# The second batch's attention turned through DRAM and multiplied by quarters of the array

## Chip, cores and metric

One core of a Trainium2 chip runs the whole program. The metric is the device time of one execution in microseconds (us); lower is better. The kernel before takes 828.4 us (median of 3 runs, 827.59 to 828.51).

## What is computed

A softmax-like attention without a score matrix, then a feed-forward layer over all its tokens (8 batches, 8 heads, 576 tokens, 64 dims a head; model width 512, inner width 2048):

```python
q_s = exp(q - max(q, axis=-1)); q_s = q_s / (sum(q_s, axis=-1) + 1e-09)
k_s = exp(k - max(k, axis=2));  k_s = k_s / (sum(k_s, axis=2) + 1e-09)
kv  = einsum('bhsd,bhse->bhde', k_s, v)
x   = einsum('bhsd,bhde->bhse', q_s, kv)        # then (4608, 512) tokens
h   = x @ w_in;  g = s * max(h, 0)**2 + b;  out = g @ w_out
```

q, k, v and w_in are drawn eight times larger than in a plain layer; everything is float32.

## The kernel before

**Attention.** The work is cut in units of two heads (`u`, four a batch) and pairs of units (`pr`, two a batch). A unit's tokens lie on 128 partitions as four full groups and a fifth, half-full one: the 64 left tokens of a head. For x, the dims of q have to lie on partitions, so q is turned. Batches 0 and 1 (`k_stream`, `k_pair`, `q_stream`, `q_left`, `kv_stream`, `kv_second`) do this on TensorE: `qT` transposes the four full groups of a unit (L543), `xp` multiplies them by `kvf` (L553), a 128x128 matrix with the two heads' kv on its diagonal blocks; the left tokens of a pair go through `qTl` (L603) and `xpl` (L610). In batch 1 the maximum of k over the tokens is also found with TensorE: `kT` turns the partial maxima (L629) and `mb` spreads the result over the partitions (L636). Batches 2 to 7 (`k_late`, `k_exps`, `q_late`, `kv_late`, `x_late`) keep those turns away from TensorE: VectorE transposes 32x32 blocks (L763), SyncE stores the result to DRAM (`turned`, L766) and loads it back in another order (L771), ScalarE and VectorE split it in a high and a low part, and `xp` is three fp32r products for each half (L830). The maxima of k go through DRAM in the same way (L679, L683).

**The layer.** For batches 0 to 4 it goes in 16 steps of 128 inner columns (`step`): `h` (L1468, 12 products of 128x512), then r, gh and gl on ScalarE and VectorE, then `acc` (L1548, 12 products of 128x512). Each of the 80 steps is 24 such products on TensorE. In the first block of steps the weights are also fetched (L291, L293) and brought into a high and a low part on ScalarE and VectorE (`conv_w`: `low`, `st`, `w`; L307 to L326). Batches 5 to 7 and the left tokens of all batches go through a scheme with seven products instead of eight (`product` L1104, `second` L1195); it is not touched.

**Order.** Every piece of work is a generator that yields an `Op` (engine, planned cost, due time, needs, buffers). A table of letters, `TURNS_TAKEN`, says which generator comes next, so the order of the instructions on each engine is fixed when the program is built; each engine works through its own list in order. Where the plan leaves TensorE idle at the start, `idle` (L1691) puts in transposes without a use (`unused`, L1702). The plan's costs are not times of the chip. SyncE issues nearly all transfers, in order: one that waits holds back all behind it.

The lines that say what a late unit does on TensorE:

```python
qs = part().rearrange("p l (s a n c) -> p l s n a c", s=2, a=2, c=SQ)
for s_, n in enumerate((NT, NQ)):
    for k, (l, m) in enumerate(((0, 0), (1, 0), (0, 1))):
        nc.tensor.matmul(xp[:, s_, 0:n * D], kv_part()[:, l, i], qs[:, m, s_, 0:n], start=k == 0, stop=k == 2)
```

Of the kernel before, what the change touches and what calls it, by code (L numbers as in the profile page):

```python
# [9 lines left out]
F32 = mybir.dt.float32  # L10
# [16 lines left out]
def attention_moe(ctx: ExitStack, tc: tile.TileContext, q, k, v, w_in, w_out, s, b, out):  # L27
# [4 lines left out]
    P = 128  # L32
# [29 lines left out]
    DUE_Q = (-17.0, -5.5, -20.5, -11.0, 8.5, 5.5, 12.5, 14.0)  # L62
    DUE_V = (-13.5, -19.0, -11.5, 14.0)
# [63 lines left out]
    class Op:  # L127
# [11 lines left out]
        "aaaaababaaaaabaaabaWabaWabaQaWaWabaQaWaQabaWaXaWaQabaXaRaQaWauaRaXabaXaWabaRaXaba8aRaXabaXavabaRabauaSavabaua8avaSabauabaSaYaoauaSa8aYaZaTaS"  # L139
        "aqauaWaYaZaYaTaXaWaYaTaZbcaYaWaYaZa9aTaXaZbcaXaTawaZaYaZaXa9awaYaXawavaZbcaZa9adbcawavaYadaxaZavaeaYaxaeacaZbcaYawaZbcbcacayawbcbcaye1axbdbc"  # L140
        "bda4bcaxbda4aybdbcafaxafa4aybdbcbdbcaxagbdbcagaUbcbdbeaUaybebda4beazayapbeaAbda4e2a4bdazbea4bdaAazbdbeaAa4bfazbfbeaAbfa4ahaza4ahbfbea4aiaDaU"
        "azbeaibfbeaDaAbebfbeaDaAbgbfbgaDe3aBbgaCbfbgakaDaBbfakaCa1bgbfaDaBbfaCbfbgaEbhaBbgbhaCbgaBbhajaCbhajaBbgaCbhe4a1bgaFbha1bga1aEbgbha1biaEbhbi"
        "a1bia1aGbiaEa1bibhaUalbiaFbhalaGbibha0bibha0a1aUbibja0aEaUbjaFaEbjbjaGaUbiaFaJbibjbiaJaUambjbiaJamaGbkbjbkaUaJanbkaFbjanbaa5aJaFa5aGbkarbaaK"
        "babjaJbaa5bjaKataGbjaKbkbjaKaHblbkaKblaHbkaKe5blaHbkblaIaHbkblaIbkaHblaIbkaHblbkaIe6a0bmblaIbma0asa5aIbmaNa0a1a0aLa5bma1a5aNblbma5a1blbmaVa0"
        "bmblaVbmblaLa0bnbmaNa0aNaLbna0bnaMa0bnaNaLa5bmaMbnaNbma5aLa5bnaMbma5aLbmbnaMe7boaObnboaMaOaPboaMaOaPboa2aPaVaObnboaVbnboaPaVboa2bnaVa2bnboaV"
        "bpaOaPbpboaVaObpaVaPbpe8a2a3bobpa2a3bobpa2boa2bpboa3bqbpa3a2bpbqa3a2bqa3a3bqbpbqeQeQbpbqbpbqbpbqa3bbbqa3brbbcubrbbbbbrcva2cwbra2bqa2brcxbqbr"
# [12 lines left out]
        "fud1dmbVbUeAd0fubWd1bWeAfubWd1fufubWfubVbWekbWeUd2bWbVd2cVekbWbVekbWbVekeUbXekdmbXbXcUdmdEbXd0dEcWbWbXd0bWdFbXd1bWd2dFbWbXd2bYbXeZbYd2bYd2bY"
# [406 lines left out]
    def q_left(pr):  # L566
# [1192 lines left out]
```

## Time and profile before

| what | value |
|---|---|
| median of 3 runs | 828.4 us (827.59 to 828.51) |
| the profiled execution, its time | 828.27 us |
| its span, first to last instruction | 826.5 us |
| TensorE busy | 817.6 us, 4301 records |
| VectorE busy | 673.3 us |
| ScalarE busy | 463.5 us |
| GpSimd busy | 205.3 us |
| granted TensorE clock | 1.00 of full speed in every slice |

PE is TensorE, DVE VectorE, ACT ScalarE, POOL GpSimd, SPq the queue of SyncE. A float32 product (not fp32r) shows as two records, so `xp` of L553, two products a unit, counts x4. The records of neighbouring products overlap, since they are pipelined: how long one keeps TensorE is read from start to start, and the chain of waits prints just that.

### The profile page before, as it was taken

Reading aid. Unit: us, or ns where it says so; the run is one execution under the profiler, and the core shown is the slowest. Engines: PE = TensorE matmul, PEld = TensorE weight load, DVE = VectorE, ACT = ScalarE, POOL = GpSimd, SP = SyncE. Lnnn points to the kernel's source line nnn. Section 1 sums busy time; section 2 is a strip of 40 time slices with the busy share of each in tenths; the row PEclk is TensorE's granted clock in tenths of the full one; section 3 lists DMA queues with packets and bytes.
Section 4 is the critical chain, followed back from the end, with each engine's and each line's share of the span. In section 5 each row is a group of like instructions: output and inputs, shape, how many; then the busy total and the mean of one; then the engine's idle time right before and its main releaser. Section 6 shows DMA issues by size and latency. Waiting matters only on the chain.

```text
span 826.5 us, 12888 instructions
## 1 busy us (share of the span) xinstructions
PE 817.6 (99%) x4301; PEld 676.7 (82%) x4301; DVE 673.3 (81%) x1155; ACT 463.5 (56%) x768; POOL 205.3 (25%) x206
## 2 busy tenths in 40 slices
PE   8999999999999999999999999999999999999997
PEld 7688888888888888888888888888888888888886
DVE  6999956799899996978979978699969976656883
ACT  4999964356446455564556555545447644445650
POOL 3100012212212122222222322335342005353500
PEclk9999999999999999999999999999999999999999
DMA  9999523587867666866695754789889967666314
GB/s 267 319 375 318 164 70 110 151 228 191 218 179 198 168 170 205 214 177 144 203 241 163 242 149 149 231 264 283 276 253 325 251 156 214 203 182 187 90 18 73
DMA packets 217206, 165.64 MB, mean 200 GB/s; under 512 B 91444, under 2 KB 200500, under 8 KB 217140
## 3 DMA queue, kind: packets, MB, share of 16 engines
q1 hardware_dynamic: 212116, 163.83, 68.6%
q10 hardware_dynamic: 5024, 0.98, 0.6%
q8 instruction: 34, 0.56, 0.3%
q14 instruction: 32, 0.26, 0.1%
HBM read 112.85 MB, written 52.44 MB: 200 GB/s over the span
## 4 chain that ended last, share of the span: by engine, by line
PE 96%; DVE 2%; issue 1%; ACT 0%; POOL 0%; POOLq 0%; ACTq 0%
PE acc L1548 27%; PE h L1468 26%; PE bankU L1104 11%; PE overX L1195 8%; PE bankV L1104 8%; PE overY L1195 5%; PE overZ L1195 5%; PE xp L830 2%; PE kv L402 2%; PE kT L440 1%; PE xp L553 1%; PE unused L1702 0%; PE bankU L1195 0%; DVE low L318 0%; DVE st L311 0%
## 5 line engine op out<-in xcount | busy, mean ns | idle before, releaser
L1468 PE MATMUL h<-x,w 128*128 128x512 f32 x960 | 238.2, 392 | 1.3 <-ACT r L1500 0.8
L1468 PEld LDWEIGHTS h<-x,w 128*128 128x128 f32 x960 | 177.9, 188 | 38.8 <-ACT r L1500 1.3
L1548 PE MATMUL acc<-w,gh 128*128 128x512 f32 x640 | 199.2, 392 | 0.0
L1548 PEld LDWEIGHTS acc<-w,gh 128*128 128x128 f32 x640 | 118.1, 188 | 23.5
L1548 PE MATMUL acc<-w,gl 128*128 128x512 f32 x320 | 125.1, 391 | 0.1
L1500 ACT ACTIVATE r<-h 128x512 f32<-128x512 f32 x80 | 47.9, 599 | 94.7 <-PE h L1468 94.1
L1104 PE MATMUL bankU<-w,ring 128*128 128x512 f32 x378 | 95.9, 389 | 0.0
L1104 PEld LDWEIGHTS bankU<-w,ring 128*128 128x128 f32 x378 | 70.9, 188 | 14.7
L1548 PEld LDWEIGHTS acc<-w,gl 128*128 128x128 f32 x320 | 60.1, 188 | 14.2 <-DVE gl L1527 0.9
L1104 PE MATMUL bankV<-w,ring 128*128 128x512 f32 x282 | 71.5, 389 | 0.0
L759 POOL TENSOR_TENSOR qe<-qe,qr 128x640 f32<-128x640 f32 x24 | 33.2, 1384 | 127.8 <-DVE qr L755 66.7
L1104 PEld LDWEIGHTS bankV<-w,ring 128*128 128x128 f32 x282 | 52.9, 188 | 11.0
L1514 DVE SCALAR_TENSOR_TENSOR h<-h,sb,r 128x512 f32<-128x512 f32 x47 | 35.3, 752 | 18.3 <-ACT r L1500 18.0
L742 POOL TENSOR_TENSOR area<-area,qm 128x640 f32<-128x640 f32 x24 | 31.2, 1300 | 74.3 <-DVE qm L740 45.4
L1516 ACT ACTIVATE gh<-h,sb 128x512 fp32r<-128x512 f32 x47 | 32.4, 690 | 28.6 <-DVE h L1514 28.5
L1195 PE MATMUL overX<-w,w 128*128 128x512 f32 (+1 forms) x177 | 40.5, 384 | 0.0
L1195 PEld LDWEIGHTS overX<-w,w 128*128 128x128 f32 x177 | 32.7, 188 | 6.5
L1518 DVE SCALAR_TENSOR_TENSOR gl<-h,sb,gh 128x512 fp32r<-128x512 f32 x47 | 34.7, 738 | 3.4 <-ACT gh L1516 3.2
L1510 DVE TENSOR_TENSOR gl<-r,gh 128x512 fp32r<-128x512 f32 x23 | 17.5, 762 | 15.6 <-ACT gh L1508 15.5
L927 DVE TENSOR_TENSOR S<-S 128x128 f32<-128x128 f32 x64 | 26.7, 418 | 0.7
L1195 PE MATMUL overZ<-gh,w 128*128 128x512 f32 x88 | 27.1, 389 | 0.0
L927 DVE TENSOR_TENSOR Z<-Z 128x128 f32<-128x128 f32 x64 | 25.2, 394 | 1.0
(329 smaller groups left out, 1524.1 us busy)
## 6 DMA issues: line engine op xcount, KB each, us to landing
ring<-aset SPq DMA_DIRECT2D x55, 512.0 KB, 4.0
w<-wset SPq DMA_DIRECT2D x80, 256.0 KB, 3.9
st<-in_moe_w_in_dram SPq DMA_DIRECT2D x16, 512.0 KB, 7.8
st<-in_moe_w_out_dram SPq DMA_DIRECT2D x16, 512.0 KB, 8.6
wset<-Z SPq DMA_DIRECT2D x32, 256.0 KB, 3.9
turned<-area SPq DMA_DIRECT2D x24, 320.0 KB, 3.6
qe<-turned SPq DMA_DIRECT2D x48, 160.0 KB, 3.5
area<-in_v_dram SPq DMA_DIRECT2D x56, 128.0 KB, 3.8
```

Of the source, the lines that this page charges most:

```text
L742: nc.gpsimd.tensor_tensor(out=qt, in0=qt, in1=bc(qm, [P, 2, NT, D]), op=ALU.subtract)
L759: nc.gpsimd.tensor_tensor(out=qe_, in0=qe_, in1=qr, op=ALU.mult)
L927: eng.tensor_tensor(out=o, in0=x, in1=y, op=op)
L1104: nc.tensor.matmul(out_, w[:, a, c * P:(c + 1) * P], slot(k, c)[:, b_], start=k in (0, 1, 3) and n == 0, stop=n == 5, skip_group_check=True)
L1195: nc.tensor.matmul(out_, w[:, l], g[m][:, cols], start=k not in (2, 4) and p == begin_ and n == 0, stop=p == end_ and n == 2, skip_group_c ...
L1468: nc.tensor.matmul(hp_, w[:, j, c, :], x[:, c, :], start=(c == 0 and i == 0), stop=(c == NP - 1 and i == 2))
L1500: nc.scalar.activation(r, hp_, AF.Relu)
L1510: nc.vector.tensor_tensor(out=gl, in0=r, in1=gh.bitcast(F32), op=ALU.subtract)
L1514: nc.vector.scalar_tensor_tensor(out=hp_, in0=hp_, scalar=s_col, in1=r, op0=ALU.mult, op1=ALU.mult)
L1516: nc.scalar.activation(gh, hp_, AF.Identity, bias=b_col)
L1518: nc.vector.scalar_tensor_tensor(out=gl, in0=hp_, scalar=b_col, in1=gh.bitcast(F32), op0=ALU.add, op1=ALU.subtract)
L1548: nc.tensor.matmul(acc[blk, j // 2][:, j % 2], g[:, js], w_, start=(f == 0 and i == 0), stop=(f == NFC - 1 and i == 2))
```

## The change

Batch 1 leaves the path of batch 0 and goes the way of batches 2 to 7 (`late` now starts at `NP // 2`), with a shorter end: what comes back from DRAM is not split. Its x is made by four float32 products of 64 by 64, each in one quarter of the array: `xp[half[h], s, ...]` from `kvf[half[s], h]` and `qs[half[s], h, ...]`, where s is the half of the tokens and h the head. So the contraction is over 64 rows, two row halves serve the two halves of the tokens, two column halves the two heads, and the two row halves write different banks. `kvf` of batch 1 therefore holds each head's kv twice (four VectorE products instead of two), and its off-diagonal blocks are cleared again by GpSimd before batch 2. The table of turns is new throughout, so the order on every engine differs from the start to about the third batch of steps and, off TensorE, further; a few operations of batch 0 change their engine.

```diff
-    KN_ON = ('ACT', 'DVE', 'ACT', 'DVE')
-    QF_ON = ('DVE', 'ACT', 'ACT', 'ACT', 'ACT', 'ACT', 'ACT', 'DVE')
+    KN_ON = ('ACT', 'ACT', 'ACT', 'ACT')
+    QF_ON = ('ACT', 'DVE', 'ACT', 'DVE', 'ACT', 'ACT', 'ACT', 'DVE')
-    SUB_ON = ('D', 'D', 'P', 'P', 'D', 'D', 'D', 'P')
-    MUL_ON = ('P', 'D', 'P', 'D', 'D', 'D', 'P', 'D')
+    SUB_ON = ('P', 'D', 'P', 'P', 'D', 'D', 'D', 'P')
+    MUL_ON = ('P', 'P', 'P', 'P', 'D', 'D', 'P', 'D')
     TURNS_TAKEN = (
-        "aaaaababaaaaabaaabaWabaWabaQaWaWabaQaWaQabaWaXaWaQabaXaRaQaWauaRaXabaXaWabaRaXaba8aRaXabaXavabaRabauaSavabaua8avaSabauabaSaYaoauaSa8aYaZaTaS"
+        "aaabaaaaaaabababababababababababababababaOaKaKaKaKaLaPaoaOaOaPaPaLaoaKaOaOaOaPaPaLaLaoapaLaoaUaOapaPaMaMaOaUaoapaMaOaQaRapaUaPaMaoaQaQaMaQap"
...
         qe = work.tile([P, 2, 2, NT, SQ], F32, name=f"qe_{u}", tag="qe", bufs=2)
-        nc.scalar.activation(qe, qt.rearrange("p h n (r t) -> p h t n r", t=2), AF.Exp)
+        quarters = u < 2 * NP
+        if quarters:
+            nc.scalar.activation(qe.rearrange("p t h n r -> p t (h n) r"), qt.rearrange("p h n (r t) -> p t (h n) r", t=2), AF.Exp)
...
-        src = turned.pop(u).rearrange("h (a r) (t e) -> h (r t) a e", r=SQ, t=2)
+        src = turned.pop(u).rearrange("(s a r) (t e) -> s (r t) a e" if quarters else "h (a r) (t e) -> h (r t) a e", **{"s": 2} if quarters else {}, r=SQ, t=2)
         t = qe.rearrange("p h t n r -> p (h t n r)")
         for h in range(2):
-            nc.sync.dma_start(t[half[h]].rearrange("p (a e) -> p a e", a=4), src[h])
+            nc.sync.dma_start(t[half[h]].rearrange("p (a e) -> p a e", a=2 if quarters else 4), src[h])
+        if quarters:
+            backs[u] = qe
+            return
...
         for h in range(2):
-            nc.vector.tensor_tensor(
-                out=kvf[half[h], :, h], in0=kv[half[h], :, 0:D], in1=z[half[h]].unsqueeze(2).to_broadcast([D, 2, D]), op=ALU.mult
-            )
+            for to in range(2) if first else (h,):
+                nc.vector.tensor_tensor(
+                    out=kvf[half[to], :, h], in0=kv[half[h], :, 0:D], in1=z[half[h]].unsqueeze(2).to_broadcast([D, 2, D]), op=ALU.mult
+                )
...
+            before = [f"kv{NP // 2 - 1}", f"ql{NP // 2 - 1}"] + [f"qe{n}" for n in range(NP - 2, NP)]
+            yield Op("PE", 0.88, due, needs=[f"q{u} back", f"kvf{pr}"] + before, take=["big"], free=["qe"], gives=[f"xp{u}"], late=SLACK)
...
+            qs = backs.pop(u).rearrange("p t h n r -> p (t h n r)").rearrange("p (a h n c) -> p h n a c", a=2, h=2, c=SQ)
+            kvf = kvfs[pr % 2][:, i]
...
         for s_, n in enumerate((NT, NQ)):
+            if bb == 1:
+                for h in range(2):
+                    nc.tensor.matmul(xp[half[h], s_, 0:n * D], kvf[half[s_], h], qs[half[s_], h, 0:n], start=True, stop=True)
+                continue
...
-    late = range(NP, NU // 2)
+    late = range(NP // 2, NU // 2)
...
-            + [x for pr in range(NP // 2, NP) for x in reload(pr)]
-            + [k_stream(u) for u in range(NP)] + [k_pair(pr) for pr in range(NP // 2, NP)]
-            + [q_stream(u) for u in range(2 * NP)] + [q_left(pr) for pr in range(NP)]
-            + [kv_stream(pr) for pr in range(NP // 2)] + [kv_second(pr) for pr in range(NP // 2, NP)]
+            + [k_stream(u) for u in range(NP)] + [q_stream(u) for u in range(NP)] + [q_left(pr) for pr in range(NP // 2)]
+            + [kv_stream(pr) for pr in range(NP // 2)]
```

Three places in the order. The first is TensorE in the first block of steps (`h_10` is the h of step 10, `xp_5` the x of unit 5). Before:

```order
L1468 MATMUL h_10_1026<-x_0_353,w_10_926 128x512 x9
L553 MATMUL xp_5_1048<-early_88,kvf_83 128x256 x2
L1468 MATMUL h_10_1026<-x_0_353,w_10_926 128x512 x3
L1548 MATMUL acc_0_0_522<-w_9_895,gh_9_1002 128x512 x2
L1548 MATMUL acc_0_0_522<-w_9_895,gl_9_1003 128x512
L1548 MATMUL acc_0_0_522<-w_9_895,gh_9_1002 128x512 x2
L1548 MATMUL acc_0_0_522<-w_9_895,gl_9_1003 128x512
L543 MATMUL qT_4_1077<-ident_78,qe_4_833 128x128 x4
```

TensorE's list around the first unit of batch 1 now:

```order
L1582 MATMUL acc_0_2_567<-w_5_690,gl_5_782 128x512
L1502 MATMUL h_7_870<-x_0_349,w_7_791 128x512 x12
L861 MATMUL xp_4_930<-qe_4_692,kvf_83 64x320 x2
L861 MATMUL xp_4_930<-qe_4_692,kvf_83 64x256 x2
L1502 MATMUL h_8_947<-x_0_349,w_8_908 128x512 x3
```

A unit of batch 1 no longer has `qT` and two products of 128x256; it has four products of 64 rows, which read `qe` as it came back from DRAM, and stands earlier, between step 7 and step 8.

The second place is SyncE's list in the first block, where weights 9 to 12 (`st_9` to `st_12`) are fetched. Before:

```order
L291 DMA st_8_531<-in_moe_w_in_dram 128x4x256
L293 DMA st_8_531<-in_moe_w_out_dram 128x1024
L375 DMA area_87<-in_q_dram 128x4x256
L376 DMA area_87<-in_q_dram 64x4x64
L889 DMA aset_103<-w_2_512 128x2x256 x2
L890 DMA aset_103<-w_3_551 128x2x256
L291 DMA st_9_616<-in_moe_w_in_dram 128x4x256
L293 DMA st_9_616<-in_moe_w_out_dram 128x1024
```

SyncE's list at the same weights now:

```order
L353 DMA xleft_98<-misc_91 128x2x64 x2
L680 DMA maxima_2_763<-sb_85 32x4x2
L292 DMA st_9_765<-in_moe_w_in_dram 128x4x256
L386 DMA area_87<-in_v_dram 128x4x64 x4
L387 DMA area_87<-in_v_dram 64x4x64
L684 DMA misc_91<-maxima_2_763 128x256
L292 DMA st_10_775<-in_moe_w_in_dram 128x4x256
L294 DMA st_10_775<-in_moe_w_out_dram 128x1024
L774 DMA turned_5_778<-area_87 128x640
L774 DMA turned_4_883<-area_87 128x640
L376 DMA area_87<-in_q_dram 128x2x256
L377 DMA area_87<-in_q_dram 64x2x64
```

The maxima and the turned q of batch 1 now stand among the fetches of the weights; copies of weights to `aset` have moved back. The third place is VectorE before the first gl, `gl_0`. Before:

```order
L563 TENSOR_TENSOR x_0_353<-xp_3_454,x_0_353 128x512
L1634 COPY sb_85<-both_463 128x2
L326 TENSOR_TENSOR w_1_469<-low0_1_397,w_1_469 128x2x512
L311 TENSOR_SCALAR st_3_258<-st_3_258 128x1024
L1523 SCALAR_TENSOR_TENSOR r_0_480<-r_0_480,sb_85 128x512
L582 TENSOR_REDUCE qml_0_497<-area_87 128x4
L318 SCALAR_TENSOR_TENSOR low0_2_452<-st_2_251,low0_2_452 128x1024
L1527 SCALAR_TENSOR_TENSOR gl_0_482<-r_0_480,sb_85,gh_0_481 128x512
```

VectorE's list up to `gl_0` now:

```order
L564 TENSOR_TENSOR x_0_349<-xp_3_456,x_0_349 128x512
L583 TENSOR_REDUCE qml_0_467<-area_87 128x4
L312 TENSOR_SCALAR st_3_145<-st_3_145 128x1024
L1668 COPY sb_85<-both_454 128x2
L583 TENSOR_REDUCE qml_1_471<-raw1_86 128x4
L319 SCALAR_TENSOR_TENSOR low0_2_434<-st_2_142,low0_2_434 128x1024
L1557 SCALAR_TENSOR_TENSOR r_0_487<-r_0_487,sb_85 128x512
L319 SCALAR_TENSOR_TENSOR low0_3_464<-st_3_145,low0_3_464 128x1024
L1561 SCALAR_TENSOR_TENSOR gl_0_489<-r_0_487,sb_85,gh_0_488 128x512
```

A second `qml` and the `low` of weight 3 now stand ahead of `gl_0`.

## Rows read from the trace of the kernel before

**Rows 1.** The page: busy share of TensorE, and the chain by engine.
```profile
PE 817.6 (99%) x4301; PEld 676.7 (82%) x4301; DVE 673.3 (81%) x1155; ACT 463.5 (56%) x768; POOL 205.3 (25%) x206
...
PE 96%; DVE 2%; issue 1%; ACT 0%; POOL 0%; POOLq 0%; ACTq 0%
```

**Rows 2.** Who TensorE waited for: us in total, times, longest.
```profile
PE unused L1702 <- POOL ident masks.py:199: 2.3, 1, 2.3
PE h L1468 <- ACT r L1500: 0.8, 1, 0.8
PE kn L453 <- ACT early L448: 0.6, 2, 0.4
```

**Rows 3.** Busy time by stretch: length, then each engine, clock, DMA share, GB/s.
```profile
0.00:33.00 33.00, 28.57 (x273) 22.89 (x273) 25.36 (x47) 21.52 (x36) 7.83 (x25) 1.00 0.99 295
33.00:104.00 71.00, 70.90 (x355) 57.80 (x356) 68.48 (x106) 67.30 (x104) 5.57 (x11) 1.00 0.86 286
104.00:128.00 24.00, 24.00 (x145) 19.84 (x144) 12.66 (x25) 14.59 (x24) 3.12 (x7) 1.00 0.33 88
```

**Rows 4.** Chain of waits, first block: start us, us, what. The pieces that go.
```profile
44.55 0.22 PE qTl L603 x2
...
46.85 0.39 PE xpl L610 x4
...
47.99 0.22 PE kT L629 x2
...
62.15 2.72 PE h L1468 x12
64.87 0.44 PE qT L543 x4
65.31 2.75 PE acc L1548 x12
68.05 0.22 PE mb L636 x2
...
88.23 0.86 PE xp L553 x4
```

**Rows 5.** Chain of waits: kv in column halves, and two h of 9 products.
```profile
117.42 0.44 PE qT L543 x4
117.86 1.32 PE kv L402 x40
119.18 2.27 PE h L1468 x9
...
186.38 2.05 PE h L1468 x9
```

**Rows 6.** Timeline of TensorE at 10 us: start, us, what; ten kT in column halves.
```profile
10.39 1.31 PE L440 MATMUL kT<-ident,area 128*64 128x128 f32 x20
11.63 0.66 PE L543 MATMUL qT<-ident,qe 128*128 128x128 f32 x4
```

**Rows 7.** Chain of waits at the end of the start, up to the first full acc.
```profile
23.78 0.81 DVE raw L455
...
30.23 1.22 DVE x L563 x2
...
33.99 0.33 DVE qml L582
34.32 1.13 DVE low L318
...
36.52 2.58 PE acc L1548 x10
```

**Rows 8.** The page's transfers: count, KB each, median us to landing.
```profile
turned<-area SPq DMA_DIRECT2D x24, 320.0 KB, 3.6
qe<-turned SPq DMA_DIRECT2D x48, 160.0 KB, 3.5
```

**Rows 9.** Who SyncE's queue waited for at the turned stores.
```profile
SPq L766 <- DVE area L763: 18.2, 7, 8.9
```

More of the change, by code (lines that the diff above doesn't have):

```diff
@@ L143, in attention_moe @@
[L143 to L146, printed above, removed]
@@ L715, in k_late @@
         k_out(pr, top)
-        yield Op("SP", 0.65, due, needs=[f"tops{pr}"] + [f"x{2 * NP - 1}"] * (pr == NP), late=SLACK, take=["mb"], free=["maxima"], kb=128, gives=[f"mb{pr}"])
+        yield Op("SP", 0.65, due, needs=[f"tops{pr}"] + [f"kept{n}" for n in range(NP // 2)] * (pr == NP // 2), late=SLACK, take=["mb"], free=["maxima"], kb=128, gives=[f"mb{pr}"])
         mb = k_in(pr)
@@ L750, in q_late @@
         yield Op("DVEp", 0.3, due)
-        nc.vector.scalar_tensor_tensor(
-            out=qs[:, :, 0], in0=qs[:, :, 0], scalar=1e-9, in1=qs[:, :, 1], op0=ALU.add, op1=ALU.add
-        )
+        ends = (qs[:, 0], qs[:, 1]) if quarters else (qs[:, :, 0], qs[:, :, 1])
+        nc.vector.scalar_tensor_tensor(out=ends[0], in0=ends[0], scalar=1e-9, in1=ends[1], op0=ALU.add, op1=ALU.add)
         qr = small.tile([P, 2, 2, NT], F32, name=f"qr_{u}", tag="qr", bufs=2)
-        nc.vector.reciprocal(qr, qs[:, :, 0].unsqueeze(2).to_broadcast([P, 2, 2, NT]))
+        nc.vector.reciprocal(qr, ends[0].unsqueeze(2 - quarters).to_broadcast([P, 2, 2, NT]))
         yield Op("POOL", 1.26, due)
@@ L787, in between @@
     def between():
-        yield Op("POOL", 0.05, NFC, needs=[f"w{NFC - 1} 2 read", f"w{NFC - 1} 1"] + [f"x{u}" for u in range(2 * NP)] + [f"left{pr} out" for pr in range(NP)], take=["w"], gives=["mid"])
+        yield Op("POOL", 0.05, NFC, needs=[f"w{NFC - 1} 2 read", f"w{NFC - 1} 1"] + [f"x{u}" for u in range(2 * NP)] + [f"left{pr} out" for pr in range(NP // 2)], take=["w"], gives=["mid"])
         spares.append(wpool.tile([P, NP * TB], F32R, name="spare", tag="w"))
@@ L794, in kv_late @@
         due = begin(pr)
-        gone = [f"x{u - 4}" for u in us] + [f"left{pr - 2} out"] if pr < NP + 2 else [f"kvhl{pr - 2}"]
-        yield Op("PE", 1.52, due - 200, needs=[f"k{u}" for u in us] + [f"v{pr} there"] + gone, take=["big"], gives=[f"kv{pr}"], late=WAIT)
+        first = pr < NP
+        gone = [f"x{u - 4}" for u in us] + [f"left{pr - 2} out"] * first if pr < NP + 2 else [f"kvhl{pr - 2}"]
+        yield Op("PE", 1.52, due if first else due - 200, needs=[f"k{u}" for u in us] + [f"v{pr} there"] + gone, take=["big"], gives=[f"kv{pr}"], late=0.0 if first else WAIT)
         kt, _, vt = tiles[pr]
-        kv = ps.tile([P, 2, 512], F32, name=f"kv_{pr}", tag="big")[:, 0, 0:2 * (D + 1)].rearrange("p (u e) -> p u e", u=2)
+        kv = ps.tile([P, 2, 512], F32, name=f"kv_{pr}", tag="big")[:, 0]
+        kv = kv[:, 0:2 * (D + 1)].rearrange("p (u e) -> p u e", u=2)
         heads(kv, by_head(kt).rearrange("p (u h) n d -> p u h n d", u=2), v_at(vt))
@@ L804, in kv_late @@
         kvf = kvfs[pr % 2]
[L805 removed]
+        yield Op("DVE", 1.2 if first else 0.6, due, needs=[f"x{u - 4}" for u in us] if pr < NP + 2 else [f"kvhl{pr - 2}"], free=["big"], gives=[f"kvf{pr}"])
         for h in range(2):
[L807 to L809 removed]
+            for to in range(2) if first else (h,):
+                nc.vector.tensor_tensor(
+                    out=kvf[half[to], :, h], in0=kv[half[h], :, 0:D], in1=z[half[h]].unsqueeze(2).to_broadcast([D, 2, D]), op=ALU.mult
+                )
+        if first:
+            return
+        if pr < NP + 2:
+            yield Op("POOL", 0.3, due)
+            for h in range(2):
+                nc.gpsimd.memset(kvf[half[h], :, 1 - h], 0.0)
         yield Op("ACT", 0.42, due, needs=["mid"] if pr == NP else [f"xp{2 * pr - 1}"])
@@ L1682, in v_ @@
         def v_():
-            yield Op("SP", 3.2, due, needs=[f"kv{pr - 1}"] + there, gives=[f"v{pr} there"], kb=576 * W256)
+            yield Op("SP", 3.2, due, needs=[f"kv{before}"] + there, gives=[f"v{pr} there"], kb=576 * W256)
             load_v(pr)
```

133 lines of the change are left out of this document (75 added, 58 removed).

## The prediction

> **What bounds the kernel now.** I first read the page's head: TensorE is busy 99% of the span, and 96% of the chain that ends last is its work; no other engine has more than 2% of it [rows 1]. So a microsecond counts only if it comes off TensorE's list or is spent by TensorE waiting. The list of its waits has next to nothing to win: 2.3 us before the identity is there, and 1.4 us in the start [rows 2]. The busy times by stretch say where the other engines stand: after 33 us TensorE has no gap worth naming; from 33 to 104 us VectorE is busy 68.48 of 71.00 us and ScalarE 67.30, because the weights are converted there; from 104 to 128 us VectorE has 11.3 us to spare [rows 3]. The granted clock is 1.00, the level of 2.4 GHz, in every one of these stretches, so a length read in one place holds in another. Last, the chain printed in order of time gives what each piece costs TensorE from start to start, with the layer's products on both sides [rows 4]: this is the view that prices the change.
>
> All sums are made against the profiled execution, 828.27 us; the median of the runs, 828.4, lies 0.1 us above it.
>
> **What goes.** Batch 1 had, on TensorE, four qT of 0.44 us (1.76), four xp of 0.86 (3.44), two each of qTl, kT and mb at 0.22 (1.32) and two xpl of 0.39 (0.78) [rows 4]: together 7.30 us. Behind such a piece the twelve products that follow take 2.75 us where they take 2.72 elsewhere [rows 4]; sixteen pieces at 0.03 are another 0.48. None of this lies beside other work of TensorE, so 7.8 us come off the list. The kv products stay, twenty a pair.
>
> **What comes.** Four units with four float32 products each, two of 320 columns and two of 256, on 64 rows and 64 columns of the array. One xp of the old kind is two products of 256 columns in 0.86 us, so 1.68 ns a column: 320 columns are 0.54 us and 256 are 0.43. How quarters run together no row shows. The lower bound is all four at once, 0.54; the upper is one after another, 1.94. The nearest rows are those of column halves: ten kT of 128 columns start 1.24 us before the next piece [rows 6], 0.124 each where one alone would be 0.215, so two of them share 0.248. Parts of the array that don't overlap do work side by side there. Two quarters of the same row half are such a pair; that row halves do the same is my extension, because they too share no part and write different banks. From kv, twenty products in 1.32 [rows 5], I take 0.066 us from one start to the next; the fourth product then starts 0.2 us after the first and ends at 0.63.
>
> To this I add what it costs to go back to whole-array products. Behind a kv the next nine products of h take 2.27 us, elsewhere 2.05 [rows 5]: 0.22. So a unit costs 0.85 us (ends 0.76 and 2.16), and four cost 3.4 us (ends 3.0 and 8.6). I keep to the low side because the rows of halves lie there.
>
> In the Trainium skill, "TensorEngine Tiling (Array Packing)", Key Properties, one rule speaks against this change: "Mode switching requires drain". Rows 5 bear it out on the way back from column halves, with the 0.22 above; on the way in, the qT ahead of kv has its usual 0.44, so I charge one side only. If the drain were paid on both sides, the sum would be 0.9 us higher, 826.1.
>
> **The start.** From 22 us to the first full acc at 36.52 the chain lies mostly on VectorE. Its list up to gl_0 now holds one qml and one low more, 0.33 and 1.13 us [rows 7], and one copy of kn less, 0.81, which ScalarE now does; the other differences up to there cancel. That is 0.65 us later for the first acc, and TensorE has nothing to put in. Against it stands that kT of unit 2 now has two useless transposes ahead of it instead of eight; if its k has landed by then, it starts up to 0.65 us earlier. No row shows that landing. I take +0.4, with ends 0 and +1.5.
>
> **New waits.** The quarter products read qe straight from the transfer, and two transfers are on the way, 3.6 us to landing for the store and 3.5 for the return [rows 8], 7.1 together. For unit 4 the order leaves, between VectorE's transpose and the product, o4, h6, o5, a kv and h7: 48 products of 0.227 (2.72 for twelve [rows 4]) and 1.54 us for kv [rows 5], 12.4 us. From that come off the 7.1, what VectorE has between gl_4 and the end of that transpose (half a w, a low of 1.13 [rows 7] and the transpose), which I estimate at 2.5 us, and SyncE's issues of the store, four loads of q and the return, which I estimate at 2. About 1 us is left, little but not negative. Queued behind a late product are all later products, and behind a late store on SyncE the fetches of weights 9 and 11 to 15. The maxima of k take the same road, and VectorE waits for them in the middle of its list, with gl_5 behind. I put 0.9 us for all this, with ends 0 and 8.
>
> The extra work beside TensorE costs nothing as long as its cover holds: the transposes and steps to the maxima on VectorE replace about as much reducing, subtracting and copying; GpSimd gets eight wide operations in a block in which it was busy 5.57 of 71 us [rows 3]; DMA was at 0.86 there, and the copies of weights that now come later make room. From 104 to 128 us DMA was at 0.33 and VectorE half idle, so what slips there is taken up.
>
> **Sum.** 828.27 - 7.8 + 3.4 + 0.4 + 0.9 = 825.2 us, 0.4% below the median. A measurement of this kernel can tell about 0.2% (1.7 us) from no change.
>
> **Rivals.**
> 1. VectorE sets the pace of the first block. For it: 96% busy from 33 to 104 us [rows 3], and its work for batch 1 that used to come after 104 us now comes sooner. Against: its total for batch 1 hardly changes, and TensorE never waited for it there [rows 2]. Then what TensorE loses before 104 us brings nothing: 4.7 of the 7.30 us (all the small turns of pair 2, the first two qT and xp, and the first kT and mb of pair 3). Left are 2.6 + 0.2 off, two quarter units on (1.7) and the start (0.4): 828.27 - 2.8 + 1.7 + 0.4 = 827.6, no change.
> 2. Turns come late, and TensorE waits at each quarter product. For it: SyncE waited 18.2 us in seven cases, once 8.9, for a transpose before it could store [rows 9], and nothing is split in between any more that would take up the delay; fetches share the queue. Against: later batches go the same road, and TensorE's list of waits does not name them [rows 2]. Without waits the sum is 824.3, so this decides from 5.8 us on, 1.45 at each of the four units. At 2 us each it is 832.3: slower.
> 3. Row halves do not run together, only the pairs of column halves: (0.54 + 0.43) times 1.15, and 0.22, is 1.34 a unit, 5.4 for four: 827.2, no change.
> 4. No quarters run together: 2.16 a unit, 8.6: 830.4, slower by a little.
>
> **Chances and range.** Forecast 0.60; rival 1 0.16; rival 2 0.10; rival 3 0.08; rival 4 0.06. That makes faster 0.60, no change 0.24, slower 0.16. The forecast's own range goes from 823.0 (quarters at 0.76, no waits, no loss in the start) to 826.7. With rivals 1 and 3 the range is 823.0 to 828.6 and leaves out 0.16 and a little of the ends.
>
> **What would show it.** Right: in the chain each quarter unit takes 0.6 to 0.9 us and the products behind it 0.2 us more than usual; TensorE's list of waits stays under 6 us with no row for the quarter products; the first full acc starts near 37 us. Wrong: quarter units of 1 us or more (rivals 3, 4); waits of h or acc for gl or for low and w on VectorE in the first block (rival 1); waits of the quarter products for qe's transfer, and SyncE's queue idle ahead of L774 while weights stand behind it (rival 2). If the first acc starts after 38 us, my sum of the start is wrong.

## Result and profile after

The changed kernel takes **840.7 us** (median of 6 runs, 839.06 to 841.83), the kernel before 828.45 us beside it: a ratio of 1.0149, 95% interval 1.0136 to 1.0162. It is 12.2 us slower, where 3 us faster was forecast. The profiled execution, at 841.83 us the slowest of the six, has a span of 840.0 us (before 826.5). The runs below find the loss in the order of the work, not in the quarters, and one of them beats the kernel before by 1.3 us.

The page of the changed kernel, its busy times and the chain by engine, which answer to [rows 1]:

```profile
PE 821.5 (98%) x4298; PEld 672.9 (80%) x4298; DVE 669.9 (80%) x1162; ACT 459.2 (55%) x758; POOL 217.1 (26%) x207
...
PE 80%; DVE 8%; DMA 5%; SPq 3%; ACT 2%; issue 2%; ACTq 0%; DVEq 0%
```

The share of TensorE has hardly moved, which is why one reads the second line: before, the chain lay on TensorE for 96%, now for 80%. VectorE, transfers and SyncE's queue hold 16% of it. TensorE's list of waits, against [rows 2] (us in total, times, longest):

```profile
PE acc L1582 <- DVE gl L1561: 4.0, 4, 2.1
PE unused L1737 <- POOL ident masks.py:199: 2.3, 1, 2.3
PE acc L1582 <- DVE gl L1544: 2.2, 3, 1.4
PE h L1502 <- ACT r L1534: 1.4, 2, 1.0
PE kn L454 <- ACT early L449: 0.9, 2, 0.5
PE xpl L611 <- ACT early L607: 0.7, 1, 0.7
PE xp L861 <- DMA qe<-turned: 0.7, 1, 0.7
```

The same three stretches as in [rows 3], with the same columns:

```profile
0.00:33.00 33.00, 28.77 (x284) 24.30 (x285) 21.61 (x40) 20.23 (x34) 11.08 (x25) 1.00 0.94 298
33.00:104.00 71.00, 65.30 (x313) 48.35 (x312) 63.59 (x100) 54.92 (x82) 14.66 (x16) 0.98 0.75 216
104.00:128.00 24.00, 22.90 (x139) 17.90 (x138) 21.94 (x43) 20.84 (x33) 3.12 (x4) 1.00 0.77 190
```

From 33 to 104 us TensorE does 65.30 us of work instead of 70.90. VectorE is *less* busy than before (63.59, 68.48 then) and DMA too (0.75, 0.86 then): nothing is full, everything waits. The work is only later: from 104 to 128 us VectorE and ScalarE are now busy where they had room.

To see where time is lost I set the start of each step's h in the two traces side by side. After minus before is 2.5 us at step 1, 3.8 at step 6, 10.2 at step 7, 11.1 at step 13, 10.4 at step 24, 13.4 at step 28, and 13.2 at the last product. So there are four places: the start, the stop between steps 6 and 7, the following steps, and one place in the second block. (TensorE's list is now shorter, so in the first block a drift that only stays level is a loss too.)

**The stop.** TensorE's timeline (start us, us, what, records, [idle <- releaser]):

```profile
70.04 0.61 PE L1582 MATMUL acc<-w,gh 128*128 128x512 f32 x2
72.78 0.59 PE L1582 MATMUL acc<-w,gl 128*128 128x512 f32 x1 [2.13 <-DVE gl L1561]
73.17 1.05 PE L1582 MATMUL acc<-w,gh 128*128 128x512 f32 x2
74.02 0.63 PE L1582 MATMUL acc<-w,gl 128*128 128x512 f32 x1
```

The wait is 2.13 us; the products behind it then start 0.425 us apart, not 0.227: the granted clock is 0.50, the level of 1.2 GHz, from 73.1 to 76.5 us. Seven products (not ten, as two expectations below have it) and a kv cost about 1.7 us more for it, as the window around them shows too (4.40 us at a mean clock of 0.61, with the columns of [rows 3]):

```profile
72.60:77.00 4.40, 4.22 (x37) 3.10 (x39) 4.39 (x6) 3.70 (x7) 0.35 (x2) 0.61 0.80 272
```

gl_5 was late because VectorE stood 2.35 us at the first subtraction of the maxima of pair 2 (L688), with gl_5 behind; their load (L684) was issued at 66.9 us and landed at 71.2. SyncE was late with it, and its list of waits from 30 to 70 us says why:

```profile
SPq L353 <- ACT misc L346: 13.5, 2, 7.2
SPq L377 <- ACT ql L592: 6.3, 1, 6.3
```

Twice SyncE stood, 13.5 us in all, at the store of the left tokens of batch 0 (`xleft`) for ScalarE's copy, with the maxima, weights, v and q of batch 1 behind. In the same stretch before, no wait of SyncE is over 1.1 us. The kernel before stands at these stores too, 17.4 us in the whole program, but where it costs nothing: its longest wait ends at 99.0 us with copies of weights to `aset` next in the list, and TensorE does not wait.

```profile
SPq L352 <- ACT misc L345: 17.4, 3, 11.5
```

Such a store belongs to no planned step of its own: `keep_left` issues it when its copy is issued.

**The quarters** did what was forecast wherever their qe was there:

```profile
90.12 0.39 PE L1582 MATMUL acc<-w,gl 128*128 128x512 f32 x1
90.44 0.76 PE L861 MATMUL xp<-qe,kvf 64*64 64x320 f32 x8
91.12 0.72 PE L1582 MATMUL acc<-w,gh 128*128 128x512 f32 x2
```

A unit holds TensorE for 0.69 us to the next start; the product ahead has 0.32 to the unit's start instead of 0.227 (0.09 more), and at the next two units, which have no wait behind them, the twelve products that follow take 2.87 instead of 2.72. That is 0.92 us a unit; 0.85 was forecast. All twelve units of order_new, order_new_2 and misc_apart take 0.69 as well. One unit of the change differs: the first waited 0.68 us for its qe and then took 1.11. So the sign of rivals 3 and 4, a unit of 1 us or more, appears once, at the one unit whose transfer was late.

### The profile page after: what moved, and what is told of

The parts are those of the page before. It is cut to its first block, busy times and chain, and to the rows that moved or that the text cites. A ratio compares the mean times of both kernels' runs of the same rounds, so it can differ in the third digit from the quotient of the medians.

```text
span 840.0 us, 12915 instructions
## 1 busy us (share of the span) xinstructions
PE 821.5 (98%) x4298; PEld 672.9 (80%) x4298; DVE 669.9 (80%) x1162; ACT 459.2 (55%) x758; POOL 217.1 (26%) x207
## 4 chain that ended last, share of the span: by engine, by line
PE 80%; DVE 8%; DMA 5%; SPq 3%; ACT 2%; issue 2%; ACTq 0%; DVEq 0%
PE acc L1582 20%; PE h L1502 19%; PE bankU L1138 10%; PE overX L1229 8%; PE bankV L1138 8%; PE overY L1229 5%; PE overZ L1229 5%; PE xp L864 2%; PE kv L403 2%; DVE low L319 1%; DMA misc<-maxima 1%; DMA st<-in_moe_w_out_dram 1%; DMA raw<-in_k_dram 1%; DMA turned<-area 1%; DVE r L1557 1%
## 5 line engine op out<-in xcount | busy, mean ns | idle before, releaser
L765 POOL TENSOR_TENSOR qe<-qe,qr 128x640 f32<-128x640 f32 x28 | 39.2, 1399 | 148.7 <-DVE qr L761 90.3
L745 POOL TENSOR_TENSOR area<-area,qm 128x640 f32<-128x640 f32 x28 | 38.4, 1372 | 89.4 <-DVE qm L743 50.6
L1548 DVE SCALAR_TENSOR_TENSOR h<-h,sb,r 128x512 f32<-128x512 f32 x47 | 35.3, 751 | 17.3 <-ACT r L1534 17.1
L961 DVE TENSOR_TENSOR Z<-Z 128x128 f32<-128x128 f32 x64 | 37.5, 587 | 1.2
L769 DVE STREAM_TRANSPOSE area<-qe 128x640 f32<-128x640 f32 x28 | 23.4, 835 | 3.5 <-POOL qe L765 3.5
```

The costliest lines, as they stand in the source:

```text
L745: nc.gpsimd.tensor_tensor(out=qt, in0=qt, in1=bc(qm, [P, 2, NT, D]), op=ALU.subtract)
L765: nc.gpsimd.tensor_tensor(out=qe_, in0=qe_, in1=qr, op=ALU.mult)
L769: nc.vector.transpose(out=tb, in_=qe.rearrange("p h t n r -> p (h t n r)"))
L961: eng.tensor_tensor(out=o, in0=x, in1=y, op=op)
L1548: nc.vector.scalar_tensor_tensor(out=hp_, in0=hp_, scalar=s_col, in1=r, op0=ALU.mult, op1=ALU.mult)
```

## Experiments

All are the changed kernel with one thing altered, unless said otherwise. A move in the order is a change of `TURNS_TAKEN` alone, and SyncE's list shows it.

**mb_first.** The load of the maxima ahead of v:

```diff
-L386 DMA area<-in_v_dram 128x4x64 x4
-L387 DMA area<-in_v_dram 64x4x64
 L684 DMA misc<-maxima_763 128x256
+L386 DMA area<-in_v_dram 128x4x64 x4
+L387 DMA area<-in_v_dram 64x4x64
```

> One transfer moved in SyncE's list: the load of the first pair's maxima (L684) goes ahead of the five loads of v (L386, L387) that now hold the queue from 59.15 to 66.76 us. Theory A (VectorE in order behind the maxima): VectorE's wait of 2.35 us for L688 goes, with it the 2.1 us in which TensorE waits for gl of step 5 and the ten products behind it that take 0.425 us instead of 0.227 (1.9 us more): 840.7 becomes 836.5 to 838. Rival B (VectorE has more work than time there; the wait only took up slack of other queues): something else is late next, 840 to 841.

Measured: 845.5 us (ratio 1.0197 to 1.0235), 4.8 slower than the change. The stop at 70 us fell from 2.1 to 0.6 us with the clock at full, so the cause of that stop was named rightly. But the first quarter product then waited 4.9 us for kvf, with the clock at 0.50 from 81.0 to 87.9. The three lists, of TensorE, VectorE (55 to 95 us) and SyncE (56 to 84 us):

```profile
PE xp L861 <- DVE kvf L823: 4.9, 1, 4.9
...
DVE qm L743 <- DMA area<-in_q_dram: 3.8, 1, 3.8
...
SPq L376 <- DMA turned<-area: 5.2, 1, 5.2
```

v was not late: kv is done at 74.0 us. VectorE stood at the first reduction of the last q (L743) with kvf behind it, and the loads of q could be issued only from 76.6 us on, as the turned store of the same tile landed. A wait taken away came back, longer, at the next late transfer: rival B's reading, but well outside its 840 to 841.

**gpsimd_small.** GpSimd does its two wide operations of batch 1's q on a fifth of the columns; the rest of q isn't subtracted or scaled.

```diff
-        nc.gpsimd.tensor_tensor(out=qt, in0=qt, in1=bc(qm, [P, 2, NT, D]), op=ALU.subtract)
+        few = 1 if u < 2 * NP else NT
+        nc.gpsimd.tensor_tensor(out=qt[:, :, 0:few], in0=qt[:, :, 0:few], in1=bc(qm[:, :, 0:few], [P, 2, few, D]), op=ALU.subtract)
...
-        nc.gpsimd.tensor_tensor(out=qe_, in0=qe_, in1=qr, op=ALU.mult)
+        few = 4 if u < 2 * NP else 4 * NT
+        nc.gpsimd.tensor_tensor(out=qe_[:, 0:few], in0=qe_[:, 0:few], in1=qr[:, 0:few], op=ALU.mult)
```

> The eight wide operations of GpSimd for batch 1 (L745 and L765, units 4 to 7) work on a fifth of their columns, so q is neither reduced by its maximum nor divided by its sum for the rest. Theory A (VectorE and GpSimd get in each other's way): VectorE's stretched operations of the first block (gl 1.42 instead of 0.68 us, r 1.75 instead of 0.73, the 64x8 step of the maxima 1.20 instead of 0.15, st 1.00 instead of 0.68, gl 1.75 instead of 0.73 near 113 us; 4.1 us together) return to their usual length, and TensorE gains 3 to 4.5 us: 836 to 838. Rival B (GpSimd is off the path and the stretches are hidden by waits for transfers): 840 to 841.

Measured: 843.0 us (1.0157 to 1.0196). Outside both expectations. At step 13 the drift against before is 7.2 instead of 11.1, 3.9 us less; but 1.0 of that is there at step 1, before GpSimd's first operation for batch 1 (42.0 us), and at step 16 only 1.5 beyond it are left. A wait of 2.1 us for gl that ends at 150.7 us and others up to 218 us took it back. So the run shows a gain of 1.5 to 2.9 us in the first block and none in time.

**gap_filled.** In step 5 the second product of the first acc is done nine times, so that TensorE works in the stop; that acc holds this term nine times.

```diff
-                nc.tensor.matmul(
-                    acc[blk, j // 2][:, j % 2], g[:, js], w_, start=(f == 0 and i == 0), stop=(f == NFC - 1 and i == 2)
-                )
+                for _ in range(9 if t == 5 and j == 0 and i == 1 else 1):
+                    nc.tensor.matmul(
+                        acc[blk, j // 2][:, j % 2], g[:, js], w_, start=(f == 0 and i == 0), stop=(f == NFC - 1 and i == 2)
+                    )
```

> In step 5 the second product of the first acc is done nine times instead of once, so TensorE has 1.8 us of products in the gap before gl of step 5 (the output holds eight of them too many). Theory C (the slow products behind the gap come from TensorE having stood still): the ten products after the gap take 0.227 us instead of 0.425, the clock row stays at 1.00 there: 1.9 us less, 838.8. Rival: the clock falls for another reason, the products stay at 0.425 and the time at 840.5 to 841.5.

Measured: 846.0 us (1.0198 to 1.0232). Outside both expectations. TensorE still waited 1.75 us there, and the clock stayed at 1.00; kvf (2.2 us) and y (1.9) were waited for later, and behind the wait for kvf the clock was at 0.50 from 82.4 to 89.2 us. So the low clock was not spared but moved. Inconclusive for its price.

**quarters_twice.** All quarter products done twice: `for h in (0, 1, 0, 1):` at L860.

> Each unit of batch 1 does its four quarter products twice, the second time over the first. Theory of the prediction (the quarters share the array, 0.6 to 0.7 us a unit): 4 x 0.65 = 2.6 us more where TensorE is the bound, 843.3; less, down to 841.5, where TensorE then only waits less for VectorE behind them. Rival (quarters run in pairs or one by one, the row of the trace deceives): 1.2 to 1.9 us a unit, 5 to 8 us more, 846 to 848.

Measured: 844.3 us (1.0183 to 1.0217), between the two expectations; the profiled span is 1.7 us longer. The time settles nothing, but the trace does. Eight products instead of four:

```profile
90.95 1.29 PE L861 MATMUL xp<-qe,kvf 64*64 64x320 f32 x16
92.17 0.73 PE L1582 MATMUL acc<-w,gh 128*128 128x512 f32 x2
```

The unit holds TensorE 1.22 us, 0.53 more, so four products go together in about the time that one of 320 columns would take (0.54, worked out in the prediction). Rivals 3 and 4 are out.

**v_early.** v's five loads ahead of the stores of left tokens, at 42 us:

```diff
+L386 DMA area<-in_v_dram 128x4x64 x4
+L387 DMA area<-in_v_dram 64x4x64
 L353 DMA xleft<-misc 128x2x64 x2
 L680 DMA maxima<-sb 32x4x2
 L292 DMA st<-in_moe_w_in_dram 128x4x256
-L386 DMA area<-in_v_dram 128x4x64 x4
-L387 DMA area<-in_v_dram 64x4x64
 L684 DMA misc<-maxima 128x256
```

> The five loads of v for the third pair go into SyncE's list right behind the weights that are issued at 42 us, where the queue now stands idle from 42.35 to 49.59 us for a store of left tokens; so they no longer hold it from 59.15 to 66.76 us, and all behind them (maxima, turned units, q, weights 10 to 13) can go up to 7 us sooner. Theory A (the queue of SyncE sets the pace of the first block): TensorE's wait of 2.1 us near 70 us goes, with the slow products behind it (1.9 us), the 0.7 us for qe, and part of the later waits for weights: 834 to 837 us. Rival B (VectorE is full from 33 to 68.9 us and late by itself): only the wait at 70 us shrinks, the rest comes back as other waits for gl: 838 to 841.

Measured: 839.2 us (1.0112 to 1.0159), 1.5 less, which is not clear of the noise, and in rival B's range. The stop at 70 us is gone (drift 4.7 at step 7 instead of 10.2), and 2.1 us come back at the first quarter product, not at gl: kvf stands in VectorE's list behind the first reduction of the last q (L743), whose load is late, as in mb_first.

**copies_early.** The copies of weights 0 to 3 to `aset` (L923, L924), which the change had moved to 170 to 190 us, go back to 41 to 47 us.

> Two of the copies of weights to DRAM (L923, L924; of weights 0 and 1, and of 2 and 3) are issued between 42 and 57 us, where DMA is nearly idle, instead of near 170 and 185 us. Theory D (the copies that the new order put into the second block hold back the loads of q there, VectorE waits 2.4 us for one, and 3.3 us are lost from step 24 to step 28): the loss there shrinks to 0 to 1 us, 837.5 to 838.5. Rival: the second block is late for other reasons, 840 to 842; if the copies hold the maxima or the weights behind them in the first block, up to 844.

Measured: 837.1 us (1.0095 to 1.0129), 3.6 better. From step 24 to step 40 the drift falls by 1.3 us (8.6 to 7.3), where in the change it rises by 2.5 (10.4 to 12.9), so the gain lies in the second block. In the changed kernel a load of q issued at 192.8 us landed at 197.2; VectorE waited 2.4 us for it, and ScalarE's S (L963) 5.0 for VectorE. The copies themselves had landed by 190.1; ahead of the load in SyncE's list stand other stores of weights too, so the run shows what the copies' place costs and not by which transfer.

**vector_less.** VectorE's share of the new way cut: batch 1's q is reduced over an eighth of its columns and a fifth of it transposed.

```diff
-        nc.vector.tensor_reduce(out=qm, in_=qt, axis=AX.X, op=ALU.max)
+        nc.vector.tensor_reduce(out=qm, in_=qt[:, :, :, 0:D // 8] if u < 2 * NP else qt, axis=AX.X, op=ALU.max)
...
-        nc.vector.transpose(out=tb, in_=qe.rearrange("p h t n r -> p (h t n r)"))
+        few = P if quarters else NT * P
+        nc.vector.transpose(out=tb[:, 0:few], in_=qe.rearrange("p h t n r -> p (h t n r)")[:, 0:few])
```

> For the four units of batch 1 VectorE reduces an eighth of q and of exp(q) and transposes a fifth of it, so the maxima, the sums and what is turned are wrong; that is about 1.9 us less of VectorE a unit, 7.5 in all, nothing else changes. Rival B (VectorE has too much to do in the first block): gl comes sooner everywhere, 834 to 836.5 us. Theory A (SyncE's queue sets the pace, VectorE waits for it anyway): less than 1.5 us, 839 to 841.

Measured: 840.4 us (1.0127 to 1.0187), no better than the change. TensorE's list now begins with a wait for a transfer:

```profile
PE xp L862 <- DMA qe<-turned: 2.9, 2, 2.3
PE acc L1583 <- DVE gl L1562: 2.7, 3, 2.2
```

Step 7 does start 4.7 us sooner than in the change (1.3 of them from the start), and by step 9 the waits for qe and a low clock have taken all but 0.4 of it back. So it isn't the amount of VectorE's work alone that sets the pace (rival 1): with less of it the transfers do.

**two_moves.** v_early and copies_early together, gl_5 ahead of the subtraction of k on VectorE, and the reduction of the last q behind kvf and gl_6.

> The changed kernel with four moves in its order and nothing else: v's five loads early as in the run v_early, the copies of weights 0 to 3 early as in copies_early, gl_5 ahead of the clearing of k on VectorE, and the subtraction of the last q unit of batch 1 (qm) after kvf and gl_6. Theory D (the loss is several separate stops, each made by a late transfer and the work that stands behind it in order): the two gains of 1.5 and 3.6 us add up, and the qm move takes away the wait of 2.1 us that v_early left: 840.7 - 1.5 - 3.6 - 2.1 = 833.5, range 831 to 835.5. Rival (each wait taken away only shows the next one, since VectorE and the queue are full in the first block): no better than copies_early alone, 836.5 to 838.

Measured: 834.8 us (1.0066 to 1.0096), in the range of theory D. Four moves of the order give 5.9 of the 12.2 us back.

**order_new, order_new_2, before_reordered.** The whole of `TURNS_TAKEN` drawn up anew, with durations of the profiles as costs; the operations and their engines stay. The first two are the changed kernel, the third is the kernel before.

> The changed kernel with its whole table of turns drawn up anew, so that the same operations stand in another order; none is added or taken away, and the engines and the quarter products are as in the changed kernel. Theory (the whole loss of 12 us beside the terms of TensorE's list is the order): the drift against before at the end of the first block is 0 or negative and the time 825 to 831. Rival (the loss lies in the work of batch 1's new way itself, on VectorE, GpSimd and the transfers in the first block, whatever the order): at least 834, no better than the two moves together.

> As order_new, with another table: a second draw of the same kind, which tells how far one table is luck. If the order is all, 825 to 832, within 3 us of order_new; if one of the two is at 836 or more, a table alone decides by as much as the whole loss and neither says what the change is worth.

> The kernel before, batch 1 still turned on TensorE, with its table of turns drawn up anew in the same manner as in order_new. It tells what a new order alone is worth. TensorE is busy 99% of the span there and waits 3.7 us in all, so an order can win little: 825 to 829. If it comes out 1 to 3 us under before, the same sum has to come off what order_new gains, and the change itself is worth the difference of the two.

Measured: order_new **827.6 us** (ratio 0.9988 to 1.0007), order_new_2 830.2 (1.0018 to 1.0037), before_reordered 829.4 (1.0006 to 1.0025). This settles the main question: the same operations cost 13.1 us less in another order, and the kernel before gains nothing from one such table. In order_new SyncE stands 3.5 us for the copies of left tokens, not 13.5. The two tables lie 0.5 us under and 2.1 over the kernel before (828.07 beside them), so by them alone the change is worth nothing that could be told from the luck of a table. order_new_2 has one stop after the start, 2.7 us from 74.8 to 77.5, and its chain of waits names it without a gap:

```profile
64.88 5.93 DMA xleft<-misc
70.80 0.02 issue
70.82 0.03 SPq L684
70.85 0.04 issue
70.89 4.45 DMA misc<-maxima
75.34 0.02 issue
75.36 0.83 DVE area L688
```

The store of left tokens was issued at 64.88, when its copy was done; SyncE then stood until it had *landed* (misc_apart below tests this reading), because the load of the maxima behind it writes the same columns of `misc`. VectorE's subtraction waits for the load, and r, gh and gl of step 7 stand behind that.

**maxima_later.** order_new_2 with VectorE and ScalarE doing first what is ready there. VectorE's list:

```diff
-L688 TENSOR_TENSOR area<-area,misc 128x640
 L327 TENSOR_TENSOR w_869<-low_8_660,w_869 128x2x512
 L319 SCALAR_TENSOR_TENSOR low_9_835<-st_693,low_9_835 128x1024
+L1557 SCALAR_TENSOR_TENSOR r_890<-r_890,sb 128x512
+L688 TENSOR_TENSOR area<-area,misc 128x640
+L1561 SCALAR_TENSOR_TENSOR gl_892<-r_890,sb,gh_891 128x512
 L688 TENSOR_TENSOR area<-area,misc 128x640
```

> order_new_2 with one place of its order changed: its profile has a single stop of TensorE after the start, 2.7 us at 74.4 us, and there VectorE stands 3.6 us at the first subtraction of the maxima of pair 2 (L688), whose load could only be issued once the store of left tokens had landed 5.9 us after its issue, because both use the tile misc. Here VectorE and ScalarE do the work that is ready first (the conversions of weights 8 and 9, r, gh and gl of step 7) and the two subtractions and exponentials of k behind it; the kv of pair 2 moves behind the first three products of the next acc. Theory (one late transfer stops TensorE only through what stands behind it in the order of VectorE): the stop at 74.4 us shrinks from 2.7 us to under 1, and the time falls from 830.2 by 1.5 to 3 us, to 827 to 829. Rival (the maxima are needed then anyway, so the wait goes over to the kv products): a wait of about 2 us ahead of kv, and the time within 1 us of 830.2.

Measured: 832.4 us (1.0029 to 1.0063, single runs from 827.8 to 835.0): a miss. The stop that order_new_2 had is gone, but then:

```profile
PE xp L861 <- DVE r L1557: 2.8, 1, 2.8
...
PE h L1502 <- ACT r L1534: 1.6, 2, 0.9
...
PE kv L403 <- POOL area L734: 1.1, 1, 1.1
```

Its window from 92.0 to 96.4 us, with the columns of [rows 3]:

```profile
92.00:96.40 4.40, 4.40 (x11) 3.43 (x12) 3.24 (x6) 3.69 (x7) 0.00 (x0) 0.50 0.94 329
```

Behind the 2.8 us the clock was 0.50 once more. (The list names VectorE's r, which that product doesn't read; what it reads, the returned qe, was issued at 81.2 and 81.8 us and took 8.8 and 8.9 to land, with DMA at 0.98 from 80 to 90 us.) The load of the maxima was issued at 72.1 us, later still than in order_new_2, with the turned stores behind it: the late transfer was still late, and the wait went to what hung on SyncE's list behind it. The profiled execution is the slowest of nine that lie 7.2 us apart, so it tells what the longest one waits for and not the median.

**misc_apart.** order_new_2, order untouched, one address changed, so that the load needn't wait for the store:

```diff
-        mb = bits[:, 0:4 * D]
+        mb = bits[:, 2 * P:2 * P + 4 * D] if pr < NP else bits[:, 0:4 * D]
```

> order_new_2, order untouched, with one address changed: the maxima of pair 2 are loaded into columns 256 to 511 of the tile misc (free again since the maxima were reduced) and not into columns 0 to 255, where the left tokens of batch 0 wait for their store. In order_new_2 the load (L684) was issued at 70.89 us, as the store of 64.88 landed, and landed itself at 75.3; VectorE stood 3.64 us for it and TensorE 2.7. Theory (the late maxima come from the shared columns: the load has to wait until the store has read them, and SyncE with it): the load is issued near 65.5 us and all that stands behind it in SyncE's list, the two turned stores among it, up to 5.5 us sooner; VectorE's wait and the stop of 2.7 us at 74.4 us are gone: 826.5 to 828.5. Rival (as in maxima_later, the next transfer takes the wait's place): a stop of 2 us or more at kv or at a quarter product before 95 us, and 829.5 or more.

Measured: **826.8 us** (ratio 0.9977 to 0.9995), 3.4 less than order_new_2, and 1.3 less than the kernel before (0.05% to 0.23%). The load was issued at 66.1 us instead of 70.9, the first turned store at 68.0 instead of 71.7. From 36 us to the end TensorE's list of waits has one row, of step 1's h, which starts at 35.6 us; the rest lies in the start:

```profile
PE h L1502 <- ACT r L1534: 0.7, 1, 0.7
```

And its page's chain by engine:

```profile
PE 96%; DMA 3%; ACT 1%; issue 0%; DVE 0%; SPq 0%
```

TensorE has 96% of the chain, as before the change. The kernel before was not run with such an address; TensorE has no wait listed behind its start there, so there is little to win.

## Why the prediction was wrong

**TensorE's list was right.** Forecast were -7.8 for what goes and +3.4 for the quarters, -4.4 us. misc_apart has nearly no waits behind the start, so it can be read there: from the start of step 1's h to the start of the last product the kernel before takes 32.96 to 821.89, 788.93 us, and misc_apart 35.59 to 820.09, 784.50. That is -4.43; ahead of step 1 both do the same work but for transposes without a use. That it fits to 0.03 is luck in part: the unit was 0.92 us instead of 0.85, 0.3 for four, and what went was worth that much more. I had charged the way back into whole-array products 0.22 and the way in nothing, where the trace has 0.15 and 0.09. With "Mode switching requires drain" (the Trainium skill, "TensorEngine Tiling (Array Packing)", Key Properties) the trace agrees on both sides, and the two sides together cost what I had put on one.

**New waits, 0.9 us: the step that failed.** In the changed kernel the same stretch takes 35.42 to 835.06, 799.64 us, 15.1 more than in misc_apart, and beyond my own upper end of 8. The lists of waits show 8.5 us of it as idle time of TensorE between 36 and 285 us; about 1.7 are the low clock, and the other 4.9 lie in many smaller pieces that no run takes apart. Three sentences of that part were wrong. First, I counted the issues in SyncE's queue, and not what SyncE would *stand* for: the two stores of left tokens were in my second place of the order, and I priced them at nothing; they held it 13.5 us, and behind them came five loads of v ahead of the maxima. Second, I took 3.6 us to landing for a turned store from a median over the program [rows 8]; the first one in the change took 6.3 (68.53 to 74.82), and I added nothing for what stood between it and the return but 2 us of issues. The next load of q goes into the tile that the store reads, so SyncE stood for its landing, with the return behind (its list from 30 to 110 us):

```profile
SPq L376 <- DMA turned<-area: 5.2, 1, 5.2
```

The issues took about 5 us: 0.4 for the store, 2.2 for the four loads, 2.3 for the return. Third, I named gl_5 as queued behind the maxima, and put no price on it of its own.

**"The copies of weights that now come later make room", and "what slips there is taken up": wrong.** They came into the second block, and copies_early measures 3.6 us for their place there.

**"The extra work beside TensorE costs nothing": too simple for GpSimd.** VectorE's operations stretch beside GpSimd's wide ones (below), and GpSimd's low busy share, my evidence, said nothing of that. Its price is not settled: gpsimd_small gains 1.5 to 2.9 us in the first block and loses them again, and in misc_apart, with the same work on GpSimd in another order, TensorE waits for nothing behind the start.

**The start, 0.4 us with ends 0 to 1.5: on the small side.** Step 1's h starts 1.8 to 2.9 us later than before in the profiles of the change and of its new tables. But the eight other profiles with the change's own order up to there have 0.7 to 2.0, six of them inside my ends, so a single profile says this only to about 1 us. The first full acc, at 36.5 in [rows 7], comes after 38 us in the change and in misc_apart, the bound I had set. In misc_apart's chain ScalarE is what ends last:

```profile
32.83 0.15 ACT st L315
32.98 0.89 issue
33.87 1.15 ACT st L315
35.03 0.52 ACT r L1534
35.55 0.04 issue
35.59 3.02 PE h L1502 x12
```

before_reordered starts 0.8 us late too, so a part may belong to the new tables. No run takes this apart; it stays open. In misc_apart's profile the 2.6 us at step 1 are why -4.4 on TensorE's list becomes -1.8 at the last product and -1.5 in the span.

**Two sums** are off besides, without weight for the forecast: the lower end of its own range adds up to 823.5, not 823.0, and rival 1's 4.7 us hold the qTl and xpl of pair 3 too, which its list leaves out.

**Rivals.** Rival 2 had the place, SyncE's queue, and the sign, but the waits came mostly at gl (6.2 us, the longest of them behind the maxima) and only 0.7 us at one quarter product, and its 2 us at four units are about half of what was lost. Rival 1 showed the sign that I had set for it, waits of acc for gl, yet vector_less says that VectorE's load isn't the cause by itself, and order_new, with all of that load, loses nothing: an in-order engine that stands behind a late transfer looks like a full one in the list of waits, and only its busy share, lower than before, tells them apart.

## What to carry to other kernels

When work moves from a bound engine to a road of transfers, price the road and not only the work: for each in-order queue write down what stands in it ahead of each new transfer, what that waits for, and whether two transfers share a buffer, so that one must land before the next can be issued. Taking away one wait often only showed the next here (mb_first, v_early, vector_less, maxima_later); the order as a whole gave 13 us back, and one shared address 3.4. Judge a change by its best order and not by the one that it comes in, and give the kernel before as many tries at an order; here it had one.

## Behaviour of the chip that I had not expected

**VectorE beside GpSimd.** Operations of VectorE with two tensor inputs often stretch while a wide operation of GpSimd is under way. VectorE's timeline in the changed kernel:

```profile
45.78 1.75 DVE L1557 SCALAR_TENSOR_TENSOR r<-r,sb 128x512 f32<-128x512 f32 x1
...
112.69 1.75 DVE L1561 SCALAR_TENSOR_TENSOR gl<-r,sb,gh 128x512 fp32r<-128x512 f32 x1
```

GpSimd's at the same times:

```profile
45.54 1.44 POOL L745 TENSOR_TENSOR area<-area,qm 128x640 f32<-128x640 f32 x1 [1.35 <-DVE qsl L597]
...
112.45 1.45 POOL L765 TENSOR_TENSOR qe<-qe,qr 128x640 f32<-128x640 f32 x1 [4.09 <-PE acc L1582]
```

Both take 0.75 us where GpSimd is idle; each ended 0.55 us after GpSimd's operation did. The Trainium skill ("GPSIMD Engine Reference", 1. Specifications) says that GpSimd's way into the memory is shared with VectorE and contended by VectorE's instructions with two inputs there; the trace agrees, and shows that the waiting counts as busy time. L1548, which reads one of its inputs from a bank that TensorE wrote, takes 0.76 us with a wide operation of GpSimd beside it and without.

**The clock after a stop.** The granted clock fell to 0.50 at stops of 1.74 us (copies_early), 2.13 (the change), 2.82 (quarters_twice) and 2.84 (maxima_later), and stayed at 1.00 behind stops of 1.75 (gap_filled), 2.20 (vector_less) and 2.72 (order_new_2). So the length of a stop does not say here whether the clock falls. Where it did, it was at 0.50 from 73.1 to 76.5 us in the change and from 90.1 to 96.9 in maxima_later, which costs half of that, about 1.7 and 3.4 us, on top of the stop.

**The landing of small stores.** The store of left tokens, 64 KB, took 5.93 us to land in order_new_2 with three fetches of weights, 512 KB each, issued 3 to 4.4 us ahead of it. The other store of this kind there, issued at 59.51 us with no transfer issued in the 3 us ahead of it, took 1.65.
